# A WaveNet convolution on one core: a table of 663 moves applied to the planned instruction order

## The chip, the cores and the metric

The kernel runs on one core of a Trainium2 chip. Its time is device time in microseconds (us), given as the median of several runs. The engines have queues of their own and run in parallel: TensorE (PE, with its weight loads as PEld), VectorE (DVE), ScalarE (ACT), GpSimd (POOL) and SyncE (SP), which here only issues DMAs. Each queue runs in the order in which the program has its instructions; between queues there are semaphores.

## The reference

A causal dilated convolution (15 taps, dilation 2) of x (2 x 16000 x 144, bf16) to 288 channels, a gate, and a product with a 144 x 144 matrix:

```python
h = jnp.einsum('btc,cd->btd', xp[:, pad:pad + T, :], w[0])
for i in range(1, K):
    off = pad - i * dil
    h = h + jnp.einsum('btc,cd->btd', xp[:, off:off + T, :], w[i])
z = jnp.tanh(h[..., :D]) * _sigmoid(h[..., D:])
return z @ w_o
```

## The kernel before

**Tiling.** The 32000 rows are cut into 128 segments of 250, one to a partition, so that one matmul does one time step of all segments: a tile of 128 channels x 128 segments (XA) against 128 x 288 weights (WA, one per tap). The other 16 channels of eight taps are stacked in a second tile (XB, weights WB). Time steps are taken in groups of eight (octets).

**Fewer matmuls.** Sums and differences take the place of some of the products. DVE forms differences of the tiles in three levels (V, DU and DD from XA, BD from XB; `tt`, line 735) and over two octets (GX, GU, GV, GD; `g_diffs`, lines 809 to 821), and sums of the weights (WC, WS, WD, WV, WT; `wsum`, line 670). A unit is one parity of a pair of octets. Its matmuls are groups of two to four into one PSUM bank (line 827, all through the helper `region` or `mm`): CV, CD and XC make common parts, XR, SR and EF the parts of one octet, DD the ends. Between the groups ACT copies a bank to a second one (`copy`, line 976) or moves a pair of banks to SBUF as UD, UC or XS (`evict`, lines 477 and 480: one instruction if the two banks are neighbours, two if not). DVE adds UD (line 1003) and in EF the shared parts UE and UX to banks (line 1077; these are called the EF additions below), and POOL adds UC and XS to UX (line 1013).

**The end of a unit.** ACT takes Sigmoid and Tanh of a finished pair of banks into TG (`halves`, through `evict`), DVE multiplies them into Z (`gate`, line 854), SP transposes Z by DMA into ZT (`ship`, line 916), PE multiplies by w_o (WOR; `project`, line 933), ACT moves the result to OS (line 876) and SP stores it (line 944).

**Loads.** SP loads x in chunks (Xr, line 519). DVE or ACT copies 128 channels to STA, which SP transposes by DMA into XA (line 700). DVE copies the other 16 to C16 (line 686); SP transposes that to T16 (line 722), writes it to a DRAM scratch and builds XB from that and from the octet before (line 712).

**The start.** x and w come in pieces by SP (lines 519, 531); two small pieces for the first partition are issued by ACT. PE transposes the first x tiles (line 622), ACT and DVE move them to XA (line 628), DVE clears the first columns (line 636), ACT compacts the 16 channels into XBc (line 588), and PE computes the first eight steps directly (`direct`, tap by tap) while DVE makes the weight sums. ACT's queue begins with its DMA issues and a Sigmoid of a small zero tile SCR (line 564) that nothing reads.

**What sets the order.** All operations are entered in a graph (`_Graph.add`) with an engine, an estimated duration and the keys they read and write. `schedule` lays them out with a list scheduler ten times over, each time with due times from the pass before, and keeps the shortest plan: an order for each engine, and a PSUM bank for each bank object. The plan kept is that of the fourth pass. It has 977 operations on PE (2553 matmuls), 670 on ACT, 652 on DVE, 85 on POOL and 276 on SP. `assign` and `plan_waits` then turn dependencies into semaphores, and `emit` writes the queues.

Of the kernel before, what the change touches and what calls it, by code (L numbers as in the profile page):

```python
# [11 lines left out]
SEM_LAT = 0.05  # L12
DMA_LAT = 2.8
DMA_RATE = 280e3
MM = 0.122
PE_WIN = 42
ORDER = ("EF0 PJ EF1 XC1 CV CD0 DD00 DD01 DD10 CD1 XR1 XC0 DD11 UP0 XR0 SR0 PJ PJ SR1 UP1", "EF0 PJ EF1 XC1 CV CD0 CD1 XC0 DD00 SR0 XR0 SR1 XR1 UP0 UP1 DD01 DD10 DD11 PJ PJ")
LAT = {"pe": 0.17, "act": 0.12, "dve": 0.08, "pool": 0.1, "sp": 0.0}


class _Op:
# [46 lines left out]
class _Graph:  # L68
# [42 lines left out]
    def schedule(self, passes=10):  # L111

        users = {}
        for op in self.ops:
            for d in op.deps | op.soft:
                users.setdefault(d, []).append(op)
        best = None
        late, hint = {}, {}
        for _ in range(passes):
            span = self.run(users, late, hint)  # L120
            if best is None or span < best[0] - 1e-6:
                best = (span, dict((e, list(o)) for e, o in self.order.items()), [(op.start, op.end, op.bdeps, [b.phys for b in op.banks]) for op in self.ops])
            hint = dict((op, op.start) for op in self.ops)
            late = {}
            seq = {}
            extra = {}
            for a, b in zip(self.order["pe"], self.order["pe"][1:]):
                seq[a] = b
            for op in self.ops:
                for d in op.bdeps:  # L130
                    extra.setdefault(d, []).append(op)
            for op in sorted(self.ops, key=lambda o: -o.start):
                t = 1e9 if not (op.eng == "pe" or op in users) else span
                for u in users.get(op, ()):
                    if op in u.deps:
                        t = min(t, late[u] - self.lag(op, u))
                for u in extra.get(op, ()):
                    t = min(t, late[u] - self.lag(op, u))
                if op.eng == "pe":
                    t = min(t, late[seq[op]] - op.dur) if op in seq else min(t, op.start)  # L140
                late[op] = t
        self.order = best[1]
        for op, (a, b, c, d) in zip(self.ops, best[2]):
            op.start, op.end = a, b
            op.deps |= set(c)
            for bk, ph in zip(op.banks, d):
                bk.phys = ph
        return best[0]
# [4 lines left out]
    def run(self, users, late, hint):  # L153
        left = dict((op, len(op.deps | op.soft)) for op in self.ops)
        avail = dict((e, []) for e in self.ENGS)
        free = dict((e, 0.8) for e in self.ENGS)
# [4 lines left out]
        pool = []  # L161
        bleft = {}
# [6 lines left out]
        fixed = dict((b.phys, b) for b in bleft if b.fixed)  # L169
# [4 lines left out]
        dma_free = 0.0  # L174
        port = {"dve": 0.0, "pool": 0.0}
        ready = {}
# [3 lines left out]
        def make(op):  # L180
            t = 0.0
            for d in op.deps:
                t = max(t, d.start + d.dur if d.eng == op.eng == "pe" else d.end + SEM_LAT)
            for d in op.soft:
                t = max(t, d.start)
            ready[op] = t
            avail[op.eng].append(op)
# [61 lines left out]
        while n < len(self.ops):  # L249
# [24 lines left out]
            if op.opens:  # L274
                pool.sort(key=lambda x: x[:2])
                bd = set()
# [21 lines left out]
            for u in users.get(op, ()):  # L298
                left[u] -= 1
                if left[u] == 0:  # L300
                    make(u)
        return max(op.end for op in self.ops)

    def needs(self, op):
# [71 lines left out]
def _conv_wavenet_kernel(nc, x, w, w_o, out):  # L376
# [39 lines left out]
    with contextlib.ExitStack() as st:  # L416
# [891 lines left out]
        store_some(o1, [7], 1, 4, 4)  # L1308
        store_some(o1, [3], 1, 4, 0)

        _ms = g.schedule()
        nsem = [0]

        def mksem(name):
# [75 lines left out]
```

## Time and profile before

| | |
|---|---|
| median of 3 runs | 311.82 us (311.77 to 312.16) |
| the profiled execution | 310.92 us, span 309.2 us |
| granted TensorE clock | 0.998 |
| PE, DVE, ACT, POOL busy | 300.3, 289.7, 258.3, 101.3 us |
| matmuls | 2553 |
| DMA | 48.48 MB, mean 157 GB/s |

The span runs from the first to the last instruction of one profiled execution. A busy time is the union of an engine's instruction records, and records can overlap: a matmul's record (0.286 us for 288 columns) lasts longer than the time to the next one. Idle time ahead of an instruction is put down to whatever it waited for last. In the time line and the chain of waits each row has a start, a length in us, an engine (SPq is SP's queue of DMA issues), a line, an operation and the tiles out<-in.

### The profile page before, as it was taken

Reading aid. Unit: us, or ns where it says so; the run is one execution under the profiler, and the core shown is the slowest. Engines: PE = TensorE matmul, PEld = TensorE weight load, DVE = VectorE, ACT = ScalarE, POOL = GpSimd, SP = SyncE. Lnnn points to the kernel's source line nnn. Section 1 sums busy time; section 2 is a strip of 40 time slices with the busy share of each in tenths; the row PEclk is TensorE's granted clock in tenths of the full one; section 3 lists DMA queues with packets and bytes.
Section 4 is the critical chain, followed back from the end, with each engine's and each line's share of the span. In section 5 each row is a group of like instructions: output and inputs, shape, how many; then the busy total and the mean of one; then the engine's idle time right before and its main releaser. Section 6 shows DMA issues by size and latency. Waiting matters only on the chain.

```text
span 309.2 us, 7467 instructions
## 1 busy us (share of the span) xinstructions
PE 300.3 (97%) x2553; PEld 235.3 (76%) x2553; DVE 289.7 (94%) x652; ACT 258.3 (84%) x812; POOL 101.3 (33%) x89
## 2 busy tenths in 40 slices
PE   8899899999999999999999999999999999999995
PEld 7677576778787777877787777877878787777874
DVE  3899799999999999999999999999999999999864
ACT  3476598788889988888988888898888889988885
POOL 7660350333332233333222333321333332133330
PEclk9999999999999999999999999999999999999999
DMA  7958656748587575857557496977927693461353
GB/s 213 294 115 158 150 148 162 140 146 197 164 160 178 124 178 155 201 169 150 180 143 159 146 168 193 145 184 147 226 86 164 158 233 88 123 139 57 99 115 118
DMA packets 100386, 48.48 MB, mean 157 GB/s; under 512 B 88285, under 2 KB 91165, under 8 KB 100347
## 3 DMA queue, kind: packets, MB, share of 16 engines
q1 hardware_dynamic: 99801, 47.62, 63.6%
q0 software_dynamic: 512, 0.33, 0.5%
q8 instruction: 20, 0.33, 0.4%
q14 instruction: 19, 0.16, 0.2%
q10 hardware_dynamic: 34, 0.05, 0.1%
HBM read 13.77 MB, written 10.20 MB: 78 GB/s over the span
## 4 chain that ended last, share of the span: by engine, by line
PE 85%; DVE 6%; SPq 3%; DMA 2%; issue 1%; ACT 1%
PE PS L827 75%; PE PS L933 9%; DMA WA<-in_w_dram 1%; DMA XB<-s 1%; DVE V L735 1%; SPq L519 1%; SPq L712 1%; DVE PS L1077 1%; DVE DD L735 1%; SPq L722 1%; DVE DU L735 1%; ACT PS L976 0%; SPq L700 0%; DVE WC L670 0%; DVE WT L670 0%
## 5 line engine op out<-in xcount | busy, mean ns | idle before, releaser
L1013 POOL TENSOR_TENSOR UX<-UC,XS 128x576 f32<-128x576 f32 x60 | 85.2, 1441 | 194.2 <-ACT UC L477 141.7
L827 PE MATMUL PS<-WA,GD 128*128 128x288 bf16 x450 | 87.3, 286 | 0.5 <-DVE PS L1077 0.5
L976 ACT ACTIVATE PS<-PS 128x288 f32<-128x288 f32 x213 | 83.0, 439 | 0.6 <-PE PS L827 0.2
L827 PE MATMUL PS<-WB,BD 128*128 128x288 bf16 x240 | 67.5, 286 | 0.0
L477 ACT ACTIVATE TG<-PS 128x288 bf16<-128x288 f32 x148 | 52.8, 425 | 14.1 <-PE PS L827 13.9
L876 ACT ACTIVATE OS<-PS 128x432 bf16<-128x432 f32 (+1 forms) x93 | 42.0, 488 | 15.0 <-PE PS L933 14.6
L827 PEld LDWEIGHTS PS<-WA,GD 128*128 128x128 bf16 x450 | 42.6, 98 | 12.9 <-DVE PS L1077 1.4
L1077 DVE TENSOR_TENSOR PS<-PS,Xp 128x288 f32<-128x288 f32 x120 | 49.7, 457 | 1.6 <-PE PS L827 0.8
L1077 DVE TENSOR_TENSOR PS<-PS,UX 128x288 f32<-128x288 f32 x120 | 49.4, 454 | 0.0
L480 ACT ACTIVATE TG<-PS 128x144 bf16<-128x144 f32 x204 | 43.7, 312 | 5.9 <-PE PS L827 5.5
L1003 DVE TENSOR_TENSOR Xp<-PS,UD 128x576 f32<-128x576 f32 x60 | 42.6, 747 | 3.0 <-ACT UD L480 2.0
L827 PE MATMUL PS<-WS,GU 128*128 128x288 bf16 x210 | 44.7, 286 | 0.6 <-DMA XB<-s 0.4
L933 PE MATMUL PS<-WOR,ZT 128*128 128x144 bf16 (+1 forms) x322 | 38.5, 253 | 0.3 <-issue 0.3
L827 PE MATMUL PS<-WB,XB 128*128 128x288 bf16 x140 | 37.6, 286 | 0.0
L827 PE MATMUL PS<-WC,GV 128*128 128x288 bf16 x210 | 35.4, 287 | 0.7 <-ACT PS L976 0.7
L933 PEld LDWEIGHTS PS<-WOR,ZT 128*128 128x128 bf16 x322 | 27.2, 98 | 5.6 <-ACT XS L477 0.6
L827 PE MATMUL PS<-WD,DD 128*128 128x288 bf16 x210 | 31.1, 287 | 0.1
L854 DVE TENSOR_TENSOR Z<-TG 128x576 bf16<-128x576 bf16 (+1 forms) x63 | 27.4, 436 | 2.1 <-ACT TG L480 1.9
L827 PEld LDWEIGHTS PS<-WB,BD 128*128 128x128 bf16 x240 | 23.5, 98 | 5.8
L827 PEld LDWEIGHTS PS<-WS,GU 128*128 128x128 bf16 x210 | 20.0, 98 | 7.4 <-ACT PS L976 1.2
L827 PEld LDWEIGHTS PS<-WD,DD 128*128 128x128 bf16 x210 | 19.5, 98 | 7.1 <-ACT PS L976 2.2
L827 PE MATMUL PS<-WT,DU 128*128 128x288 bf16 x120 | 24.5, 286 | 0.0
(92 smaller groups left out, 470.1 us busy)
## 6 DMA issues: line engine op xcount, KB each, us to landing
Xr<-in_x_dram SPq DMA_DIRECT2D x15, 576.0 KB, 4.6
out_dram<-OS SPq DMA_DIRECT2D x30, 288.0 KB, 2.4
XB<-XB SPq DMA_DIRECT2D x30, 192.0 KB, 2.8
XB<-s SPq DMA_DIRECT2D x59, 32.0 KB, 1.9
s<-T SPq DMA_DIRECT2D x30, 32.0 KB, 3.5
WA<-in_w_dram SPq DMA_DIRECT2D x2, 288.0 KB, 4.5
ZT<-Z SPq DMA_TRANSPOSE x32, 2.9
Xp<-in_x_dram SPq DMA_DIRECT2D x2, 252.0 KB, 4.3
```

The costliest lines, as they stand in the source:

```text
L477: return e.activation(bass.AP(t[:].tensor, off + (0 if st > 0 else n), [[row, NP], [st, 2], [1, n]]), bass.AP(PS[:].tensor, lo * 512 + c0, ...
L480: ins = e.activation(bass.AP(t[:].tensor, off + i * n, [[row, NP], [1, n]]), bass.AP(PS[:].tensor, q.phys * 512 + c0, [[8 * 512, NP], [1, ...
L519: return e.dma_start(tile_ap, src)
L735: return g.add("dve", lambda v: v.tensor_tensor(dst(), a(), b(), ALU.subtract), r=r, w=wk, dur=dur, prio=2, lock=True)
L827: return lambda t: t.matmul(bank(b), lhsT=lhs(), rhs=rhs(), start=start, stop=True, skip_group_check=True)
L854: g.add("dve", lambda v: v.tensor_tensor(dst(), TG[:, s, 1, 2 * k:2 * k + n, :], TG[:, s, 0, 2 * k:2 * k + n, :], ALU.mult), r=[("TG", s, ...
L876: return (lambda e: e.activation(dst(), src(), ACT.Copy)) if eng == "act" else (lambda e: e.tensor_copy(dst(), src()))
L933: return t.matmul(PS[:, c0:c0 + n * D], lhsT=ZT[:, zt, blk_, :], rhs=WOR[:, wi_:wi_ + n, :].rearrange("p a b -> p (a b)"), start=first, st ...
L976: g.add("act", lambda e: e.activation(bank(c), bank(b), ACT.Copy), r=[("bank", b)], w=[("bank", c)], dur=0.29, prio=prio)
L1003: return v.tensor_tensor(ue(u % NU, q, 0, 2).rearrange("p (v n) -> p v n", v=2), src, UD[:, u % NUD, :, :], ALU.add)
L1013: op = g.add("pool", lambda p: p.tensor_tensor(UX[:, u % NU, h, :, :], UC[:, 0, :, :], bass.AP(XS[:].tensor, h * N2, [[2 * N2, NP], [0, 2] ...
L1077: g.add("dve", lambda e, dst=dst, src=src, ua=ua: e.tensor_tensor(bank(dst), bank(src), ua(), ALU.add), r=[("bank", src), ("UX", us, h) if ...
```

## The change

`schedule` runs five passes in place of ten, which includes the fourth, so that the plan to start from is the same. A new method `replay` takes a table with one list of numbers per engine. A pair "p q" takes the operation at place p out of that engine's queue and puts it in again at place q; pairs are applied one after the other: 198 on PE, 88 on ACT, 221 on DVE, 11 on POOL and 145 on SP. `replay` then walks through the queues in the new order with the estimated durations and deals the PSUM banks anew, taking neighbouring banks for a pair where it can. The dependencies through reused banks are now those of the new dealing. No operation is added or removed.

After the moves DVE's queue begins (with the place of before in brackets): 1 to 5 the first XA moves and clearings (2, 3, 6, 4, 8), 6 a sum WD<-WA (17), 7 V (10), 8 WS (7), 9 clearing (19), 10 WC (13), 11 WC (5), 12 WC (9), 13 V (21), 14 V (12), 15 WD (37), 16 WS (14), 17 WD (11). The three differences GX, GU and GV of the first pair of octets go from 57, 58 and 60 to 60, 63 and 65, among the two BD (64, 69 to 61, 71) and the first DU and V of the next octets. The operations up to place 75 are the same ones as before. On ACT the Sigmoid of SCR goes from place 3 to 24, behind the first `halves` (19 to 21), and the compaction copy of line 588 becomes the first activation, ahead of the second small DMA issue. On PE the last `direct` groups of the larger taps and some of the first `direct` groups are put off by up to 24 places, and the transposes of the last x piece and of XBc come earlier. On SP an XB copy (22 to 17) goes ahead of the first T16 transpose; later on stores and ZT transposes go back by up to eleven places and T16, STA and XB transfers come forward. Past the first 55 us most moves are by one place on PE and ACT, and by one to nine on DVE.

```diff
--- before.py
+++ after.py
@@ -12,10 +12,59 @@
 SEM_LAT = 0.05
 DMA_LAT = 2.8
 DMA_RATE = 280e3
+FIRST = (1.12, 1.1)
 MM = 0.122
 PE_WIN = 42
 ORDER = ("EF0 PJ EF1 XC1 CV CD0 DD00 DD01 DD10 CD1 XR1 XC0 DD11 UP0 XR0 SR0 PJ PJ SR1 UP1", "EF0 PJ EF1 XC1 CV CD0 CD1 XC0 DD00 SR0 XR0 SR1 XR1 UP0 UP1 DD01 DD10 DD11 PJ PJ")
 LAT = {"pe": 0.17, "act": 0.12, "dve": 0.08, "pool": 0.1, "sp": 0.0}
+MOVES = {
+    "pe": (
+        "6 5 7 12 8 7 10 15 12 11 19 16 18 21 18 39 26 20 22 28 22 46 22 41 23 22 24 36 29 24 25 29 25 28 25 27 30 47 30 42 30 37 35 30 36 31 40 32 34 48 34 43 "
+        "41 34 38 35 37 39 38 41 39 38 47 40 42 41 43 49 44 46 50 45 47 46 49 51 62 50 52 51 53 57 53 58 57 56 72 71 76 75 78 77 80 82 85 81 82 85 84 83 94 91 "
+        "97 96 99 98 101 100 103 102 107 106 108 110 117 115 118 116 124 127 128 131 130 129 132 137 136 135 154 153 171 170 174 173 195 194 200 197 201 200 "
...
+    ),
+    "act": (
+        "4 2 4 24 6 4 8 5 7 10 12 16 12 15 18 13 14 18 20 19 25 22 24 32 28 25 28 26 29 28 30 35 30 37 30 32 36 34 39 38 41 40 49 48 51 50 55 54 57 56 61 60 63 "
+        "62 68 67 70 69 73 72 75 74 76 78 79 81 91 90 97 96 104 103 112 111 118 117 125 124 139 138 154 153 181 180 191 190 215 214 223 222 232 234 238 237 275 "
...
+    ),
+    "dve": (
+        "1 27 5 3 5 11 5 8 16 6 7 12 18 9 10 17 10 14 12 10 20 13 14 16 37 15 16 26 18 17 19 21 20 29 22 20 37 22 32 23 24 31 45 25 26 30 28 27 29 50 30 29 36 "
+        "32 37 33 37 34 41 35 44 37 40 57 43 41 45 43 50 44 47 58 51 48 59 51 61 53 56 54 63 55 57 62 57 60 58 63 62 59 61 65 63 61 64 68 65 64 72 67 69 68 71 "
...
+    ),
+    "pool": (
+        "12 19 12 22 12 15 12 14 13 24 16 13 23 16 23 17 22 18 19 21 23 22 "
+    ),
+    "sp": (
+        "22 17 21 20 23 25 26 24 26 25 28 27 30 29 36 38 44 49 46 44 47 45 48 47 54 50 51 53 54 52 54 53 55 58 55 61 56 59 56 58 57 64 59 57 61 60 65 62 65 64 "
+        "68 78 68 70 71 69 71 70 75 73 79 75 78 82 83 79 81 80 82 85 83 86 87 84 87 86 88 91 88 92 93 90 92 96 94 93 95 100 96 95 101 97 100 98 100 102 106 101 "
...
+    ),
+}
 
 
 class _Op:
@@ -142,7 +191,6 @@
         self.order = best[1]
         for op, (a, b, c, d) in zip(self.ops, best[2]):
             op.start, op.end = a, b
-            op.deps |= set(c)
             for bk, ph in zip(op.banks, d):
                 bk.phys = ph
         return best[0]
@@ -299,6 +347,89 @@
                 left[u] -= 1
                 if left[u] == 0:
                     make(u)
+        return max(op.end for op in self.ops)
+
+    def replay(self, moves):
+
+        users = {}
+        for op in self.ops:
+            for d in op.deps | op.soft:
+                users.setdefault(d, []).append(op)
+        for e, text in moves.items():
+            seq, nums = self.order[e], [int(x) for x in text.split()]
+            for p, q in zip(nums[::2], nums[1::2]):
+                seq.insert(q, seq.pop(p))
+        left = dict((op, len(op.deps | op.soft)) for op in self.ops)
+        ready = dict((op, 0.0) for op in self.ops)
+        bleft, last, fixed = {}, {}, set()
+        for op in self.ops:
+            for b in op.banks:
+                bleft[b] = len(b.ops)
+                if b.fixed:
+                    fixed.add(b.phys)
+                else:
+                    b.phys = None
+        pool = [(0.0, ph, None) for ph in range(8) if ph not in fixed]
+        free = dict((e, 0.8) for e in self.ENGS)
+        port = {"dve": 0.0, "pool": 0.0}
+        pos = dict((e, 0) for e in self.ENGS)
+        dma_free = 0.0
+        for _ in range(len(self.ops)):
+            pick = None
+            for e in self.ENGS:
+                if pos[e] == len(self.order[e]):
+                    continue
+                op = self.order[e][pos[e]]
+                if left[op] or len(pool) < len(op.opens):
+                    continue
+                t = max(free[e], ready[op])
+                if op.opens:
+                    pool.sort(key=lambda x: x[:2])
+                    t = max(t, pool[len(op.opens) - 1][0])
+                elif op.lock:
+                    t = max(t, port["pool" if e == "dve" else "dve"])
+                if pick is None or t < pick[0]:
+                    pick = (t, e, op)
+            assert pick, "the moves leave no order"
+            st, e, op = pick
+            pos[e] += 1
+            op.start = st
+            if op.lock:
+                port[e] = st + op.base
+            bd = set()
+            for b in op.opens:
+                can = [i for i, q in enumerate(pool) if q[0] <= st + 1e-9] or [0]
+                free_ph = set(pool[i][1] for i in can)
+                if b.mate is not None and b.mate.phys is not None:
+                    good = [i for i in can if abs(pool[i][1] - b.mate.phys) == 1]
+                elif b.mate is not None:
+                    good = [i for i in can if pool[i][1] - 1 in free_ph or pool[i][1] + 1 in free_ph]
+                else:
+                    good = [i for i in can if pool[i][1] - 1 not in free_ph and pool[i][1] + 1 not in free_ph]
+                _, b.phys, old = pool.pop((good or can)[0])
+                if old is not None:
+                    bd.update(old.ops)
+            op.bdeps = bd
+            op.dur, op.lat = op.base, op.base + LAT[op.eng]
+            if op.pair and len(op.banks) == 2 and abs(op.banks[0].phys - op.banks[1].phys) != 1:
+                op.dur += 0.07
+                op.lat += 0.07
+            free[e] = st + op.dur
+            if op.dma:
+                dma_free = max(dma_free, st + op.dur) + op.nbytes * (FIRST[0] if op.quick else 1.0) / DMA_RATE
+                op.end = dma_free + DMA_LAT - (FIRST[1] if op.quick else 0.0)
+            else:
+                op.end = st + op.lat
+            for b in op.banks:
+                last[b] = max(last.get(b, 0.0), op.end)
+                bleft[b] -= 1
+                if bleft[b] == 0:
+                    pool.append((last[b] + SEM_LAT, b.phys, b))
+            for u in users.get(op, ()):
+                left[u] -= 1
+                ready[u] = max(ready[u], op.start if op in u.soft and op not in u.deps else op.start + op.dur if op.eng == u.eng == "pe" else op.end + SEM_LAT)
+        for op in self.ops:
+            op.deps |= set(op.bdeps)
         return max(op.end for op in self.ops)
 
     def needs(self, op):
@@ -1308,7 +1439,8 @@
         store_some(o1, [7], 1, 4, 4)
         store_some(o1, [3], 1, 4, 0)
 
-        _ms = g.schedule()
+        g.schedule(5)
+        _ms = g.replay(MOVES)
         nsem = [0]
 
         def mksem(name):
```

26 rows, old and new, of the table MOVES are left out of this document.

## Prediction

> **What bounds the kernel now.** First the page, for the shares; then the windows view, for where the two full engines idle; then the chain, the time lines and the waits for what each idle time waits on.
>
> ```profile
> span 309.2 us, 7467 instructions
> PE 300.3 (97%) x2553; PEld 235.3 (76%) x2553; DVE 289.7 (94%) x652; ACT 258.3 (84%) x812; POOL 101.3 (33%) x89
> PE 85%; DVE 6%; SPq 3%; DMA 2%; issue 1%; ACT 1%
> ```
>
> PE is busy 97% of the span and is 85% of the chain that ended last. VectorE (DVE) is at 94%, nearly as full. The change removes no instruction of either, so all that it can win is idle time, and all that it can lose is new idle time. The windows view says where idle time is (start:end, length, then busy time and instructions of PE, PEld, DVE, ACT, POOL):
>
> ```profile
> 0.00:9.07 9.07, 7.79 (x80) 6.69 (x80) 2.50 (x13) 3.48 (x8) 5.92 (x10) 1.00 0.78 220
> 9.07:37.57 28.50, 25.73 (x217) 19.19 (x215) 26.36 (x64) 17.43 (x40) 11.97 (x20) 1.00 0.73 174
> 37.57:55.00 17.43, 16.42 (x132) 11.87 (x131) 16.98 (x36) 15.19 (x51) 6.74 (x5) 1.00 0.63 158
> 55.00:165.00 110.00, 110.00 (x931) 86.81 (x930) 108.99 (x243) 96.78 (x311) 35.07 (x26) 1.00 0.67 164
> 165.00:175.00 10.00, 9.87 (x84) 7.63 (x82) 10.00 (x23) 8.80 (x34) 2.77 (x2) 1.00 0.56 173
> 175.00:290.00 115.00, 115.00 (x973) 90.62 (x972) 113.68 (x249) 102.51 (x325) 35.17 (x26) 1.00 0.65 147
> 290.00:304.00 14.00, 14.00 (x132) 11.25 (x130) 9.80 (x27) 12.38 (x43) 3.66 (x3) 1.00 0.35 87
> 304.00:309.20 5.20, 1.47 (x21) 1.21 (x18) 1.37 (x4) 1.74 (x5) 0.00 (x0) 0.86 0.46 172
> ```
>
> PE idles 1.28 us up to 9.07, 28.50 - 25.73 = 2.77 up to 37.57, 1.01 up to 55, then 0.13 in the whole of 55 to 304, and 3.73 at the end. So 250 of the 309 us have no PE idle time to win. A short stall can hide in a busy row, because a matmul's record is longer than its place in the queue. The chain repeats two stretches in the steady part, one of 61 matmuls and one of 55, and these show how much that is:
>
> ```profile
> 118.41 7.52 PE PS L827 x61
> 172.69 7.70 PE PS L827 x61
> ...
> 200.38 6.74 PE PS L827 x55
> 272.24 6.86 PE PS L827 x55
> ```
>
> The same work differs by 0.18 and 0.12 us at most between its repeats. With some 26 such stretches and most of them within 0.06 of the shortest, I estimate about 0.8 us of hidden stalls from 55 to 304.
>
> DVE idles 28.50 - 26.36 = 2.14 us from 9.07 to 37.57, then 0.45, 1.01, 0.00 and 1.32 up to 290. It too is almost never free, and the pipeline cannot start before DVE's chain of weight sums and differences is through. Its queue in the start, with the two stalls that matter (start, length, engine, line, operation, [idle before]):
>
> ```profile
> 6.06 0.30 DVE L670 TENSOR_TENSOR WC<-WA 128x288 bf16<-128x288 bf16 x1
> 6.29 0.29 DVE L670 TENSOR_TENSOR WS<-WA 128x288 bf16<-128x288 bf16 x1
> 6.52 0.29 DVE L670 TENSOR_TENSOR WC<-WC,WA 128x288 bf16<-128x288 bf16 x1
> 6.73 0.28 DVE L735 TENSOR_TENSOR V<-XA 128x256 bf16<-128x256 bf16 x1
> 6.93 0.30 DVE L670 TENSOR_TENSOR WD<-WA 128x288 bf16<-128x288 bf16 x1
> 7.15 0.28 DVE L735 TENSOR_TENSOR V<-XA 128x256 bf16<-128x256 bf16 x1
> 9.07 0.46 DVE L670 TENSOR_TENSOR WC<-WA 128x576 bf16<-128x576 bf16 x1 [1.64 <-DMA WA<-in_w_dram]
> ...
> 31.97 0.42 DVE L735 TENSOR_TENSOR DU<-XA 128x512 bf16<-128x512 bf16 x1 [0.70 <-DMA XA<-STA]
> 34.10 0.69 DVE L735 TENSOR_TENSOR BD<-XB 128x1024 bf16<-128x1024 bf16 x1 [0.80 <-DMA XB<-s]
> 34.71 0.46 DVE L1077 TENSOR_TENSOR PS<-PS,Xp 128x288 f32<-128x288 f32 x1
> 36.34 1.22 DVE L1077 TENSOR_TENSOR PS<-PS,Xp 128x288 f32<-128x288 f32 x3
> ```
>
> **The change, part by part.** The profiled execution took 310.92 us with a span of 309.2; the median of the three runs is 311.82, 0.90 more. I work the sum against 310.92 and add the 0.90 at the end.
>
> *DVE's queue in the start (moves 5->11, 16->6, 37->15, 45->25 and their neighbours).* A WD sum that reads the third piece of WA goes to place 6. In the time line that piece lands at 9.07, so DVE now waits there. Behind it are the six sums and differences that ran from 6.06 to 7.43 while the piece was on its way. So 7.43 - 6.06 = 1.37 us of DVE work moves from before the landing to after it. Up to the third of the first EF additions (36.34, place 75 before and after) DVE has the same operations in both orders. From 9.07 to there it was busy 26.36 and idle 2.14; it now has 26.36 + 1.37, and it is earlier only by what it saves of the 2.14: at best 2.14 - 1.37 = 0.77. For that it must lose the waits of 0.70 and 0.80. I think it does: the differences GV, GU and GX, which stood ahead of these waits, now stand among them (places 58 to 65), so DVE comes to each load later in its work and finds it landed. I take -0.7. The ends are -0.77 (no idle time left) and +1.37 (all 2.14 stay).
>
> *PE's queue in the start.* It has three stalls ahead of the first EF, and two in the filling of the pipeline:
>
> ```profile
> 9.84 0.61 PE L622 MATMUL PS<-ID,Xp 128*128 128x128 bf16 x8 [0.56 <-DMA Xp<-in_x_dram]
> 11.06 4.83 PE L827 MATMUL PS<-WA,XA 128*128 128x288 bf16 x38 [0.61 <-DVE XA L636]
> 23.19 0.91 PE L827 MATMUL PS<-WC,V 128*128 128x288 bf16 x6 [0.43 <-ACT PS L976]
> 34.13 0.42 PE L827 MATMUL PS<-WS,GU 128*128 128x288 bf16 x2 [0.40 <-DMA XB<-s]
> ...
> 47.16 0.42 PE L827 MATMUL PS<-WA,GD 128*128 128x288 bf16 x2 [0.25 <-DVE PS L1077]
> 54.31 0.54 PE L827 MATMUL PS<-WC,GV 128*128 128x288 bf16 x3 [0.67 <-ACT PS L976]
> ```
>
> The moves 19->16 and 26->20 put direct matmuls and a later group of transposes into the first two, and 62->50 a DU group into the third. PE then reaches the region of 31 some 1.6 us sooner. That is worth nothing by itself: the groups there read GX, GU and GV, which DVE now makes later (places 60, 63, 65), and the second XB load, which lands at 34.1. So what PE wins before 31 it waits for after it, and the first EF additions move by DVE's term alone. I cost these moves at 0 beyond it. If DVE did not hold it back, PE could win all of 2.77.
>
> *The filling, 37.57 to 55.* PE's idle time is 1.01, of which 0.25 + 0.67 = 0.92 are two waits on places in other queues. At 47.16 it waits for an EF addition, and the moves 117->115 and 118->116 put two DD groups ahead of two EF groups there. At 54.31 it waits for a copy on ACT behind two evictions, and 76->78, 79->81 and 132->137 reorder ACT and PE there. A row of 38 matmuls in 4.83 us is 0.127 each with the last one's tail, and a single record lasts 0.29, so each of the two hides up to 0.16 more: 0.92 + 0.32 = 1.24, with the rest some 1.4. I take -1.0, between 0 and -1.4: the moves stand at these two places, but a stall that goes leaves the next queue's head to be waited for.
>
> *The steady part, 55 to 304.* Some 130 of PE's 198 moves swap neighbours here (a DD, CD, EF or SR group one place earlier), with matching moves on ACT. The idle time to win is 0.13 and the hidden stalls about 0.8. DVE has 2.33 idle there, so it could follow. Against it, every swap is fitted to a plan and could make a stall where there is none. I take -0.3, between -0.8 and +1.0 (a stall such as the 0.25 at 47.16 in four of the units).
>
> *ScalarE's first function.* Move 4->24 takes the small Sigmoid of line 564 from ahead of all other activations to place 24, behind the first real Sigmoid.
>
> ```profile
> 2.11 1.28 ACT L564 ACT_TABLE_LOAD   x1 [2.11 <-issue]
> 3.41 0.23 ACT L564 ACTIVATE SCR<-SCR 128x32 bf16<-128x32 bf16 x1
> 4.21 0.31 ACT L588 ACTIVATE XS<-Xp 128x128 bf16<-128x128 bf16 x1 [0.58 <-DMA Xp<-in_x_dram]
> ...
> 21.21 1.62 ACT L477 ACTIVATE TG<-PS 128x288 bf16<-128x288 f32 x5 [1.38 <-PE PS L827]
> 30.22 0.71 ACT L477 ACTIVATE TG<-PS 128x288 bf16<-128x288 f32 x2 [1.98 <-PE PS L827]
> ```
>
> The one table load of the program stands directly ahead of its first activation, in time that ACT had free. Now the first activation is the copy of line 588, which waits for x until 4.21, and the load may come only after that wait: 1.28 us more for the eviction behind it, which PE's direct groups read next. If what is loaded for a copy holds no Sigmoid, a second load stands ahead of the first Sigmoid (21.21 in this trace). I cost both at 0: the first is covered by PE's later wait for x (0.56 + 0.61), the second by ACT's waits for PE (1.38 and 1.98). Without that cover each costs up to 1.28. The Trainium skill's page "ScalarE: Activation LUTs", section "Table sets: the hidden batching unit", says that cheap functions sit in every set while each set has one expensive anchor, which speaks against this move, since a copy then need not bring Sigmoid along. Its section "What ACT_TABLE_LOAD costs" puts a switch at 1.28 us and 1.38 of drain; by that the whole sum would be 0.7 us above zero if nothing hid it. The trace agrees on the 1.28 and shows no drain (the activation follows 0.02 us after the load); a second load no row here shows.
>
> *The rest.*
>
> ```profile
> 12.25 8.55 POOL L1213 DMA_DIRECT2D WOR<-in_w_o_dram  x16 [0.27 <-DMA WA<-in_w_dram]
> 36.22 0.41 PE L933 MATMUL PS<-WOR,ZT 128*128 128x144 bf16 x3 [0.32 <-issue]
> ```
>
> POOL's 11 moves reorder sixteen loads that are all issued by 20.8 and first read at 36.22: 0. SP's 145 moves put the stores later and the transposes (T, XA) and XB loads earlier. In the start an XB copy goes ahead of the first T transpose and waits there for ScalarE's XB eviction; that eviction is moved up as well, so I cost it at 0, and its worst is inside the +1.37. The tail past 304 keeps its work: 0. An eviction from two banks takes one instruction if the banks are neighbours and two if not, and the banks are dealt anew; no row says how, so it stands as part of the +1.0.
>
> The sum: -0.7 - 1.0 - 0.3 = -2.0. That is 308.9 for a profiled execution and, with the 0.90, **309.8** as median.
>
> **The rivals.** (1) *PE is not held by DVE.* The deferred matmul groups fill the wait for XB, and PE loses its idle time from 9.07 on: 2.77 + 1.01 + 0.13 = 3.91, so 307.9, and down to 306.5 with the hidden stalls. For it: PE is 85% of the chain. Against: GX, GU and GV come later on a full DVE. (2) *The table loads land on the path.* One of 1.28 uncovered on top of the forecast: 311.1. For it: PE already waits 0.43 for ACT at 23.19. Against: ACT's 1.98 of waiting soon after. (3) *Slower: DVE starts its chain late.* The wait for WA at place 6 leaves 1.37 us of work behind, the waits on XA and XB stay because SP's chain is no earlier, and the first EF additions and all behind them come 1.37 later: 313.2. It decides as soon as DVE's idle time from 9.07 to those additions stays above 0.77. (4) *The table changes nothing that counts*: 250 us have no idle time to win, and what the start wins is waited for again: 311.8.
>
> **How the numbers follow.** Forecast 0.38 (308.9 to 310.6), rival 1 0.20, rival 2 0.17 (310.6 to 311.7), rival 3 0.20 (312.5 to 314.5), rival 4 0.05. The measurement can tell about 0.2%, 0.62 us, from no change. Faster by that means below 311.2: the forecast, rival 1 and half of rival 2, 0.66. Within it: the other half and rival 4, 0.14. Slower: 0.20. For 8 in 10 the range has to reach into rival 1 and rival 3: 306.8 to 313.4 leaves out the lower part of the one and the upper part of the other, some 0.15.
>
> **What would show it.** In the profile after, DVE should idle from about 6.6 to 9.07, then hardly at all up to the first EF additions, which should start near 35.6 instead of 36.34. PE's waits of 0.56, 0.61 and 0.43 should be gone, and a longer one stand ahead of its first GU or GV group. From 55 on PE should stay without idle rows, and the last matmul come 2 us sooner. I am wrong if the EF additions come later than 36.3 (rival 3), if a second table load is followed by a PE wait on ACT (rival 2), or if PE reaches them without waiting (rival 1).

## The result and the profile after

| | before | after |
|---|---|---|
| median (6 runs each) | 311.79 us (310.70 to 312.62) | 309.18 us (308.45 to 309.61) |
| ratio of after to before, 95% interval | | 0.9915 [0.9891, 0.9939] |
| the profiled execution | 310.92 us, span 309.2 | 308.45 us, span 306.4 |

The change makes the kernel 2.6 us faster; the forecast was 309.8 (306.8 to 313.4). The profiled executions differ by 2.47, and the one of after is its fastest of six.

Of the page of after, the span, the busy times and the chain of waits by engine:

```profile
span 306.4 us, 7439 instructions
PE 299.6 (98%) x2553; PEld 235.2 (77%) x2553; DVE 289.5 (94%) x652; ACT 260.0 (85%) x799; POOL 99.6 (33%) x89
PE 88%; ACT 4%; DVE 2%; DMA 2%; SPq 2%; issue 1%; DVEq 0%
```

The work is the same. Of the 2.8 us of span, 2.1 are idle time of PE (309.2 - 300.3 = 8.9 before, 306.4 - 299.6 = 6.8 after), and 0.7 was hidden in its busy time. PE's share of the chain rises from 85 to 88%, DVE's falls from 6 to 2%. ACT has 13 instructions fewer (812 before): 14 evictions less are split in two, and there is one table load more. The windows view (start:end, length, busy time and instructions of PE, PEld, DVE, ACT, POOL), with the cut of 37.57 moved to 36.50, since the pipeline starts that much sooner:

```profile
0.00:9.07 9.07, 7.69 (x77) 6.84 (x78) 2.09 (x9) 2.84 (x4) 5.93 (x10) 1.00 0.79 216
9.07:36.50 27.43, 25.94 (x221) 19.32 (x219) 26.70 (x68) 19.51 (x48) 11.47 (x21) 1.00 0.73 176
36.50:55.00 18.50, 17.99 (x146) 12.90 (x146) 18.22 (x40) 15.76 (x54) 7.13 (x5) 1.00 0.74 168
...
301.00:306.40 5.40, 1.93 (x25) 1.43 (x23) 1.70 (x5) 1.78 (x6) 0.00 (x0) 0.88 0.43 164
```

PE's idle time is now 1.49 in the start after 9.07 (2.77 before) and 0.51 in the filling (1.01). DVE is busy for 26.70 of 27.43. The time line of DVE in the start, at the places quoted for before:

```profile
8.19 0.46 DVE L801 TENSOR_TENSOR WD<-WA 128x576 bf16<-128x576 bf16 x1 [1.25 <-DMA WA<-in_w_dram]
...
33.36 0.47 DVE L1208 TENSOR_TENSOR PS<-PS,Xp 128x288 f32<-128x288 f32 x1 [0.27 <-PE PS L958]
...
35.20 1.18 DVE L1208 TENSOR_TENSOR PS<-PS,Xp 128x288 f32<-128x288 f32 x3
```

DVE waits for WA as forecast, and the waits of 0.70 on XA and 0.80 on XB are gone. The row of EF additions that the prediction goes by starts at 35.20 instead of 36.34 (it is the second of the four, where the prediction says the third). But the piece of WA landed at 8.19, 0.88 earlier than in the trace of before, and no move touches its load. From landing to second addition it is 27.01 against 36.34 - 9.07 = 27.27 before: behind the landing the order won 0.26 in these two traces. The time line of PE, its rows with idle time ahead of the first EF:

```profile
12.85 1.15 PE L958 MATMUL PS<-WA,XA 128*128 128x288 bf16 x8 [0.36 <-DVE XA L767]
20.85 0.53 PE L958 MATMUL PS<-WC,V 128*128 128x288 bf16 x3 [0.29 <-ACT PS L1107]
31.97 0.30 PE L958 MATMUL PS<-WS,GU 128*128 128x288 bf16 x1 [0.31 <-ACT PS L1107]
35.71 0.42 PE L958 MATMUL PS<-WA,GD 128*128 128x288 bf16 x2 [0.42 <-DVE PS L1208]
```

Of the three stalls of 0.56, 0.61 and 0.43 the first is gone and the other two are 0.36 and 0.29. The longer wait that I expected ahead of GU is 0.31; it seems that the groups that were put off fill most of it.

For the parts further on busy time is too coarse, so here is a measure that the text uses from now on. **Lost time** is the sum, over successive matmuls, of the time between their starts beyond the spacing that the shape has when nothing holds it (0.1225 us for 288 columns, 0.0625 for 144, 0.0555 for a transpose, read off undisturbed stretches). It is worked out from the starts of all 2553 records and shows the hidden stalls too.

| lost time of PE, us | 37.5 to 60 | 60 to 300 |
|---|---|---|
| before | 1.86 | 1.85 |
| after | 1.31 | 0.71 |

Between these two traces the filling won 0.55 and the steady part 1.1. A coarser look says the same; the windows view for 55 to 300, before and then after:

```profile
55.00:300.00 245.00, 244.87 (x2068) 192.94 (x2067) 238.99 (x527) 217.15 (x699) 76.52 (x56) 1.00 0.64 153
```

```profile
55.00:300.00 245.00, 245.00 (x2079) 193.82 (x2077) 239.80 (x530) 219.10 (x690) 75.08 (x55) 1.00 0.66 153
```

Eleven more matmuls start in the same 245 us; at 245 / 2079 = 0.118 each that is 1.3 us. ACT does it with 690 instructions instead of 699.

Last, ScalarE's table loads, in the time line of ACT:

```profile
4.23 1.28 ACT L719 ACT_TABLE_LOAD   x1 [4.23 <-DMA Xp<-in_x_dram]
5.52 0.31 ACT L719 ACTIVATE XS<-Xp 128x128 bf16<-128x128 bf16 x1
...
17.96 0.41 ACT L608 ACTIVATE TG<-PS 128x288 bf16<-128x288 f32 x1
18.39 1.28 ACT L608 ACT_TABLE_LOAD   x1
19.69 0.71 ACT L608 ACTIVATE TG<-PS 128x288 bf16<-128x288 f32 x2
```

Both loads that the prediction had thought of came: the first only after the wait for x, the second between the first gate function and the next. In this execution the second even stands on the chain of waits.

### The profile page after: what moved, and what is told of

Read it like the earlier page. It is cut to its first block, busy times and chain, and to the rows that moved or that the text cites. A ratio compares the mean times of both kernels' runs of the same rounds, so it can differ in the third digit from the quotient of the medians.

```text
span 306.4 us, 7439 instructions
## 1 busy us (share of the span) xinstructions
PE 299.6 (98%) x2553; PEld 235.2 (77%) x2553; DVE 289.5 (94%) x652; ACT 260.0 (85%) x799; POOL 99.6 (33%) x89
## 4 chain that ended last, share of the span: by engine, by line
PE 88%; ACT 4%; DVE 2%; DMA 2%; SPq 2%; issue 1%; DVEq 0%
PE PS L958 78%; PE PS L1064 9%; DMA WA<-in_w_dram 1%; SPq L650 1%; DMA XB<-s 1%; ACT TG L608 1%; ACT STA L826 1%; ACT PS L1107 1%; ACT TG L611 1%; ACT XB L792 0%; ACT L608 0%; PE PS L1024 0%; SPq L853 0%; SPq L843 0%; DVE WC L801 0%
## 5 line engine op out<-in xcount | busy, mean ns | idle before, releaser
L1144 POOL TENSOR_TENSOR UX<-UC,XS 128x576 f32<-128x576 f32 x60 | 83.8, 1417 | 191.5 <-ACT UC L608 130.4
L1107 ACT ACTIVATE PS<-PS 128x288 f32<-128x288 f32 x213 | 80.9, 429 | 2.6 <-PE PS L958 2.3
L608 ACT ACTIVATE TG<-PS 128x288 bf16<-128x288 f32 x164 | 58.3, 423 | 7.0 <-PE PS L958 6.5
L1007 ACT ACTIVATE OS<-PS 128x432 bf16<-128x432 f32 (+1 forms) x93 | 43.1, 489 | 17.0 <-PE PS L1064 15.4
L958 PEld LDWEIGHTS PS<-WA,GD 128*128 128x128 bf16 x450 | 41.8, 98 | 14.1 <-DVE PS L1208 2.0
L611 ACT ACTIVATE TG<-PS 128x144 bf16<-128x144 f32 x172 | 36.9, 304 | 5.7 <-PE PS L958 5.4
L1064 PE MATMUL PS<-WOR,ZT 128*128 128x144 bf16 (+1 forms) x322 | 41.0, 253 | 0.0
L958 PE MATMUL PS<-WC,GV 128*128 128x288 bf16 x210 | 36.5, 286 | 0.2 <-ACT PS L1107 0.2
L958 PE MATMUL PS<-WD,DD 128*128 128x288 bf16 x210 | 32.5, 286 | 0.0
```

Of the source, the lines that this page charges most:

```text
L608: return e.activation(bass.AP(t[:].tensor, off + (0 if st > 0 else n), [[row, NP], [st, 2], [1, n]]), bass.AP(PS[:].tensor, lo * 512 + c0, ...
L611: ins = e.activation(bass.AP(t[:].tensor, off + i * n, [[row, NP], [1, n]]), bass.AP(PS[:].tensor, q.phys * 512 + c0, [[8 * 512, NP], [1, ...
L958: return lambda t: t.matmul(bank(b), lhsT=lhs(), rhs=rhs(), start=start, stop=True, skip_group_check=True)
L1007: return (lambda e: e.activation(dst(), src(), ACT.Copy)) if eng == "act" else (lambda e: e.tensor_copy(dst(), src()))
L1064: return t.matmul(PS[:, c0:c0 + n * D], lhsT=ZT[:, zt, blk_, :], rhs=WOR[:, wi_:wi_ + n, :].rearrange("p a b -> p (a b)"), start=first, st ...
L1107: g.add("act", lambda e: e.activation(bank(c), bank(b), ACT.Copy), r=[("bank", b)], w=[("bank", c)], dur=0.29, prio=prio)
```

## The experiments

Twelve kernels, each timed 5 to 12 times beside before. They ran in three sets, on a chip each: the parts, the single moves, and the kernels with other banks. The median of before was 311.7, 311.9 and 311.6 in them, so kernels of different sets are compared by their ratios. The theory (T) was the one of the prediction: the start, the filling and the steady part win separately, and the new dealing of banks costs or wins little. The first rival was that something goes with the dealing, the second that single moves in the start carry the gain.

A number of use throughout is how many evictions are **split**, that is, find their two banks not neighbours and take two ACT instructions. Counted in the traces, it is 144 before, 147 in e_empty and 130 after (an expectation below gives 147 for before, which is the count of e_empty).

| kernel | split | ACT instr. | median us | ratio to before, 95% |
|---|---|---|---|---|
| e_empty | 147 | 815 | 311.77 | 0.9998 [0.9982, 1.0014] |
| e_start | 170 | 839 | 313.11 | 1.0042 [1.0025, 1.0059] |
| e_fill | 166 | 834 | 311.46 | 0.9991 [0.9980, 1.0003] |
| e_steady | 194 | 862 | 312.79 | 1.0038 [1.0023, 1.0052] |
| e_start_fill | 171 | 840 | 310.76 | 0.9964 [0.9951, 0.9978] |
| e_start_banks | 116 | 785 | 312.34 | 1.0022 [1.0011, 1.0033] |
| e_steady_banks | 125 | 793 | 311.20 | 0.9993 [0.9973, 1.0012] |
| e_split_more | 196 | 865 | 311.12 | 0.9979 [0.9958, 1.0000] |
| e_sig_first | 130 | 798 | 309.29 | 0.9924 [0.9905, 0.9942] |
| e_wd_back | 130 | 799 | 308.82 | 0.9901 [0.9881, 0.9921] |
| e_both | 130 | 798 | 308.99 | 0.9909 [0.9888, 0.9929] |
| e_late_sig | 147 | 816 | 311.87 | 0.9999 [0.9982, 1.0016] |

### The parts one by one

Each list is cut at the places of about 37 and 55 us (PE 88 and 145, ACT 45 and 85, DVE 75 and 110, SP 40 and 66; POOL's moves all belong to the start), and only one part is kept. e_empty keeps none, so that only the banks are dealt anew.

```diff
 MOVES = {
-    "pe": ( ... 198 pairs ...
+    "pe": ( only the pairs of the part; e_empty: " "
```

> The empty table: the plan of before, with the banks dealt anew by the walk through the queues. The theory expects no difference that can be measured from before, 311.2 to 312.4, with the start, the waits near 47 and 54 us and the steady part as before. The rival of the banks expects a gain of 1 us or more here, with fewer ScalarE instructions in the line of two-instruction evictions.

> Only the moves up to the first EF additions (PE places below 88, ACT 45, DVE 75, SP 40, all of POOL): 142 of the 663. The theory (three separate gains: start, filling, steady part) expects the additions at L1208 near 35.2 us as with the whole table, a last matmul 1.1 us sooner than before, and a time of 310.7. The rival that the gain comes from the new dealing of the PSUM banks expects the time of the whole table, 309.2, or that of the empty table, whatever the moves.

> Only the moves between the first EF additions and about 55 us: 55 of the 663. The theory expects 0.5 to 1.0 us less than before, 311.0, with the PE waits near 47 and 54 us shorter and all of the start as before. The rival (the wait at 54 us comes from the start's lateness) expects no gain without the start's moves, 311.8.

> Only the moves past 55 us: 466 of the 663. The prediction's term was -0.3; the two traces put the PE time lost between matmuls from 60 to 300 us at 1.9 before and 0.7 after, so the theory now expects -1.2, 310.6. The rival, that those hidden stalls went with the banks or with the better start, expects 311.5 or more.

The new dealing alone changes nothing in the time (0.9998), as T had it. The rest did not come as T had it: against 311.7 the start costs 1.4, the filling wins 0.25 (its interval holds no change), and the steady part costs 1.1. The sum is 2.2 **slower**, and the whole is 2.6 faster. So as times they are not three separate gains. In the profile of e_start the EF additions that were expected at 35.2 start at 36.16 (WA landed at 9.26 there). The waits view shows one reason for the start (window 37 to 60; engine, tile, line <- what it waited for: us in total, times, longest), in e_start:

```profile
PEld PS L931 <- DVE PS L1181: 2.7, 3, 1.1
PE PS L931 <- DVE PS L1181: 1.8, 3, 0.8
```

Line 1181 are the EF additions. With the new start and the old queues behind it PE waits for them in the filling (the two rows overlap, since a matmul and its weight load wait together; lost time 3.84 against 1.86 before and 2.74 in e_empty). For the steady part alone the waits view shows another engine; window 60 to 300, before, e_steady and after:

```profile
PEld PS L827 <- ACT PS L976: 2.9, 14, 0.4
```

```profile
PEld PS L944 <- ACT PS L1093: 4.8, 20, 0.4
```

```profile
PEld PS L958 <- ACT PS L1107: 1.1, 5, 0.3
```

These are PE's waits for `copy`. e_steady has the order of after there and waits four times as long. What differs is the dealing, with 194 splits and 862 ACT instructions against 130 and 799, and whatever stands ahead of 55 us.

### The start's single moves

e_sig_first is the whole table with the first Sigmoid ahead of all activations as before; e_wd_back puts the six short weight sums and V differences ahead of the WD sum that waits for WA; e_both does both; e_late_sig has, of the whole table, only the late Sigmoid.

```diff
 e_sig_first:  act + "3 2 24 3"    dve + "27 1"
 e_wd_back:    dve + "11 6 9 7 12 8 10 9 17 10 15 11"
 e_late_sig:   act = "4 2 4 24"    dve = "1 27"    all others " "
```

> The whole table, but ScalarE's queue begins as before: the small Sigmoid (and its DVE clearing) ahead of the copy of x. One table load near 2.1 us, none near 18.4. The theory that both loads are covered expects no change from the whole table, 309.2 within 0.6, with PE's wait for a copy near 20.3 us (0.45) smaller or gone and the time given back before the first EF additions, which stay near 35.2. The rival, that the loads cost on the path, expects up to 1.28 us less, 307.9.

> The whole table, but DVE runs the six short sums and differences ahead of the WD sum that waits for the third piece of WA, as before. DVE then has 1.37 us less to do after that piece has landed. The theory, that DVE's chain sets the first EF additions, expects them up to 1.37 us sooner, near 34.0, and a time up to 1.3 less, 308.0. The rival, that the XB loads by way of SP set them, expects them near 35.2 still, and 309.2.

> Both of these edits on the whole table. If both costs are on the path, they add up: 306.8. If ScalarE's loads are covered and DVE's chain is what counts, 308.0, as with the DVE edit alone. If neither is, 309.2.

> The empty table, with the copy of x ahead of the small Sigmoid and that Sigmoid at place 24 of ScalarE's queue: the table load's two places in an order that is otherwise that of before. The theory that ScalarE's free time covers both loads expects the time of the empty table, 311.8. The rival that they land on the path expects 1.28 more, 313.1; the wait of 0.43 for a copy at 23.19 would then be some 1 us longer.

**The loads cost nothing that shows.** e_sig_first has one load, e_late_sig two; ACT's time line of e_sig_first:

```profile
2.11 1.28 ACT L690 ACT_TABLE_LOAD   x1 [2.11 <-issue]
...
18.90 1.01 ACT L603 ACTIVATE TG<-PS 128x288 bf16<-128x288 f32 x3
```

The three gate functions run in one piece, and the time is 309.29 against 309.18 with both loads. The same pair with the short sums first, e_both and e_wd_back, is at 308.99 and 308.82. The other way round e_late_sig has 0.9999 and e_empty 0.9998, and its wait for a copy, which was expected to grow by 1 us, is 0.53 against 0.42 in e_empty. The intervals of each pair leave room for some 0.7 to 0.9 us, less than one load. That the load was on the chain of one execution did not make it worth 1.28: other waits take its place.

**The wait for WA costs at most a little, and varies.** DVE's time lines of e_sig_first and then of e_wd_back:

```profile
9.50 0.46 DVE L796 TENSOR_TENSOR WD<-WA 128x576 bf16<-128x576 bf16 x1 [2.29 <-DMA WA<-in_w_dram]
...
36.20 1.19 DVE L1203 TENSOR_TENSOR PS<-PS,Xp 128x288 f32<-128x288 f32 x3
```

```profile
8.98 0.46 DVE L796 TENSOR_TENSOR WD<-WA 128x576 bf16<-128x576 bf16 x1 [0.30 <-DMA WA<-in_w_dram]
...
34.79 0.76 DVE L1129 TENSOR_TENSOR Xp<-PS,UD 128x576 f32<-128x576 f32 x1 [0.28 <-PE PS L953]
35.46 1.18 DVE L1203 TENSOR_TENSOR PS<-PS,Xp 128x288 f32<-128x288 f32 x3
```

With the WD sum first, the additions follow the landing by 36.20 - 9.50 = 26.70 here and by 27.01 in after. With the short sums first it is 35.46 - 8.98 = 26.48. In e_both it is 35.88 - 9.42 = 26.46. So taking the 1.37 us of work out from behind the landing brings the additions some 0.5 closer to it, not 1.37. What stops them is in the second trace: DVE waits for PE, and PE's time line there says for what.

```profile
33.84 0.42 PE L953 MATMUL PS<-WS,GU 128*128 128x288 bf16 x2 [0.33 <-DMA XB<-s]
```

It is the XB load, which SP issued at 31.23 in e_wd_back and at 31.05 in after (31.44 in before). In these traces DVE's chain and SP's chain end within a few tenths of each other; after's own chain of waits, too, runs through the XB load issued at 31.05. The time of e_wd_back is 308.82, the best measured, but its interval and that of after overlap: the two are not told apart. e_both does not add the two edits up either: 308.99, where that had meant 306.8.

### Banks and parts together

Now the banks were taken by themselves. e_split_more has the order of after and takes the last fitting bank in place of the first; the other two have the order of a part alone and a dealing with few splits, taken from a table of choices; e_start_fill has the start and the filling together.

```diff
 e_split_more:
-                _, b.phys, old = pool.pop((good or can)[0])
+                _, b.phys, old = pool.pop((good or can)[-1])
 e_start_banks, e_steady_banks:
-                _, b.phys, old = pool.pop((good or can)[0])
+                cho = good or can
+                _, b.phys, old = pool.pop(cho[deal.get(nth, 0) % len(cho)])
```

> The whole table in its order, with one edit in the dealing of banks: of the free banks that fit, the walk takes the one freed last in place of the one freed first. 196 evictions of a pair of banks then need two ScalarE instructions in place of 130. The theory that the parts lost because of the dealing (170 and 194 such evictions with the start's and the steady part's moves alone, 147 before) expects most of the gain to go, 310.7 or more, with PE waiting on ScalarE. The theory that the order counts, and the parts are fitted to each other, expects 309.2 to 309.8.

> The moves past 55 us alone, in the same order as in the run of that part, with the banks dealt so that 125 evictions need two instructions in place of 194. The theory of the dealing expects the part's gain to come out: 310.6, and the time lost between matmuls from 60 to 300 us to fall from 2.8 to 0.7. The theory of the order expects 312.8 still.

> The moves up to the first EF additions alone, in the same order as in the run of that part, with 116 evictions of two instructions in place of 170. The theory of the dealing expects 311.0 or less. The theory of the order, that DVE's queue behind the start is now the wrong one for where DVE stands, expects 313.1 still, with PE waiting on DVE's EF additions between 37 and 60 us.

> The moves up to about 55 us (start and filling, 197 of the 663), banks dealt by the unchanged walk (171 evictions of two instructions). The theory of the order expects PE's lost time from 37.5 to 60 us to fall from 3.8, as with the start alone, to the 1.3 of the whole table, and 310.8: the filling's moves put DVE's queue right for the new start. The theory of the dealing expects nearly the time of the start alone, 312.5 or more.

**The dealing carries much of the gain.** e_split_more has after's order on every engine, and 66 splits more. It takes 311.12: of the 2.6 us it loses 1.9. The groups view of it, for the length of a whole eviction and of a piece of a split one (ahead of the last bar: busy, mean ns):

```profile
L603 ACT ACTIVATE TG<-PS 128x288 bf16<-128x288 f32 x114 | 42.1, 429 | 5.6 <-PE PS L953 5.3
L606 ACT ACTIVATE TG<-PS 128x144 bf16<-128x144 f32 x272 | 56.4, 322 | 7.0 <-PE PS L953 6.6
```

One record of 0.43 becomes two of 0.32, but records overlap. From start to start, back to back, a whole takes 0.305 and a piece 0.171 (medians), so a split costs ACT 2 x 0.171 - 0.305 = 0.04 of queue time. That fits its busy time, which grows by only 2.7 for the 66 (262.7 against 260.0, still 85%). My reading is that PE waits longer where such pieces stand ahead of a `copy` that it needs. The waits view of e_split_more, 60 to 300, against 1.1 in after:

```profile
PEld PS L953 <- ACT PS L1102: 4.1, 18, 0.3
```

and its windows view from 55 to 300, with 2065 matmuls where after has 2079:

```profile
55.00:300.00 245.00, 244.96 (x2065) 191.14 (x2063) 238.74 (x525) 220.11 (x740) 75.92 (x55) 1.00 0.66 153
```

e_steady_banks shows it from the other side: the steady part alone, with 125 splits in place of 194, goes from 312.79 to 311.20, and PE's waits for `copy` from 4.8 to 2.0.

```profile
PEld PS L968 <- ACT PS L1117: 2.0, 10, 0.3
```

That takes back all that the steady part alone had cost, but it is no gain over before (0.9993). What the two kernels with another dealing change is the whole dealing: which evictions are split, and also which bank waits for which. The price of a split by itself is not isolated by them.

**The start needs the filling's order, not banks.** e_start_banks has only 116 splits. It is some 0.6 us better than e_start (1.0022 against 1.0042), but still slower than before, at 312.34. Its waits view, 37 to 60:

```profile
PEld PS L956 <- DVE PS L1206: 2.7, 3, 1.1
PE PS L956 <- DVE PS L1206: 2.2, 4, 0.8
```

They are the waits of e_start, hardly changed. With the filling's 55 moves added and 171 splits, e_start_fill takes 310.76, and of these waits this is left:

```profile
PEld PS L933 <- DVE PS L1183: 0.8, 3, 0.4
```

By the ratios start and filling together win 1.1 of the 2.6 us, and the steady moves with the banks that come with them the other 1.5.

**Where each part wins and loses.** The traces of all kernels, by stretch, with the splits that fall into the last one:

| lost time of PE, us | order past 55 us | 37.5 to 60 | 60 to 300 | splits from 60 to 300 |
|---|---|---|---|---|
| before | old | 1.86 | 1.85 | 130 |
| e_empty | old | 2.74 | 1.65 | 130 |
| e_start | old | 3.84 | 2.50 | 145 |
| e_start_banks | old | 3.69 | 1.77 | 98 |
| e_fill | old | 1.73 | 2.39 | 148 |
| e_start_fill | old | 1.32 | 2.31 | 152 |
| e_steady | new | 2.78 | 2.78 | 179 |
| e_steady_banks | new | 2.47 | 1.02 | 109 |
| e_split_more | new | 1.94 | 1.97 | 167 |
| after | new | 1.31 | 0.71 | 115 |

Against e_empty, which has the old order and the same rule of dealing, the filling's moves take 1.0 off in their own stretch without the new start (2.74 to 1.73), and the steady moves take 0.6 off in theirs where few evictions are split (1.65 to 1.02 in e_steady_banks; e_start_banks, with fewer splits still and the old order, has 1.77). The start brings the EF additions nearer to WA's landing (26.90 in e_start, 27.76 in e_empty). What undoes this in the time of e_fill and e_start stands further on, where they moved nothing: 0.7 and 0.85 more from 60 to 300, with 148 and 145 splits in place of 130, and for e_start 1.1 more in the filling. So the parts do win in their own stretches. What does not add up is what a part does behind itself, through DVE's place in its queue and through the dealing. From 60 to 300 the old order loses 1.65 to 1.85 with up to 130 splits and 2.31 to 2.50 with 145 to 152, the new one 0.71 to 1.02 with 109 to 115 and 1.97 to 2.78 with 167 and more. That speaks for the splits as the way in which the dealing acts, though it does not prove it. One caution: the filling of before has 1.86 and the three kernels with its order there and a new dealing 2.47 to 2.78, yet the time of e_empty is that of before; one trace each does not say why.

## Why the prediction was right, and where it was not

**What bounds the kernel** held: all that was won is waiting of PE, 2.1 us of it visible as idle time and 0.7 hidden in busy rows. In the steady part nearly all of it was hidden.

**DVE's queue in the start (-0.7).** The mechanism was right (WD waits for WA, the waits for XA and XB go in after, the EF additions come sooner). In the profiles they came 1.14 sooner, but 0.88 of that is WA's landing, which is luck: in the traces of all kernels it lies between 8.19 (after) and 9.50 (e_sig_first). From the landing to the second addition it is 26.51 to 28.02, mean 27.51, in the six kernels with the old start and 26.70 to 27.28, mean 26.97, in the six with this one. That is some 0.5, with groups that overlap, so the term was of the right kind and somewhat too large. What it left out is a second bound: e_wd_back and e_both moved the work back, and the XB load by way of PE held the additions instead. Rival 3 did not come, since DVE lost its 1.5 us of waits; its price of 1.37 counts the moved work in full, and the 0.5 of e_wd_back makes that look too high as well.

**PE's queue in the start (0 beyond DVE's term).** Right in the sum: PE waits 0.42 for DVE ahead of the EF group at 35.71. It had less to wait out before that than I thought, it seems because it worked on deferred groups. Rival 1, PE free of DVE with 307.9, did not come.

**The filling (-1.0).** Lost time there fell by 0.55 between before and after, inside the range given. As repairs of the old stalls the moves do win 1.0 there (e_fill against e_empty), but 0.7 of it is lost again further on, and the time of e_fill is at most 0.6 below before. What I did not see is that they are also the follow-up of the new start: with it they take away 2.5 us (3.84 to 1.32).

**The steady part (-0.3, -0.8 to +1.0).** This is the term that was mis-sized: -1.1 by lost time, beyond the range on the winning side. The estimate of 0.8 for the hidden stalls looked only inside the repeated stretches. The quickest of those lose nothing (0.00 in the stretch of 61 at 118.41); much of the 1.85 from 60 to 300 stands between them, 0.29 of it ahead of one group at 169.2. And I put the new dealing of banks down only as a part of the +1.0. It was a gain: 14 splits fewer than before, 41 fewer than what the start and the filling leave with the plain dealing. From 60 to 300 e_split_more loses 1.26 more than after with 52 splits more; at that rate the 37 that e_start_fill has more than after there are worth 0.9 of the 1.6 between these two. By the rows of the old order, 2.31 with 152 splits and 1.65 to 1.85 with 130, it is nearer 0.5. Both are estimates that take splits to be alike and to be the cause; the rest, 0.7 to 1.1, would be the order.

**The table loads (0).** Right: both came, and both are covered. Rival 2 with its 1.28 is out by e_sig_first and e_late_sig, to within the 0.3% of these comparisons. The Trainium skill's page "ScalarE: Activation LUTs", section "What ACT_TABLE_LOAD costs", adds a drain to the 1.28; it shows in no row here: the activation starts 0.02 us after the second load.

**The tail (0).** From the last matmul's start to the end it is 3.63 us against 3.95, but the lost time from 300 to that matmul is 0.29 against 0.05. The end as a whole is nearly level.

So the 2.0 came out near the measured 2.6 with terms that were off both ways: between the two profiles the start behind the landing won 0.26 where 0.7 was forecast, the filling 0.55 for 1.0 and the steady part 1.1 for 0.3. Those three make 1.9, and the early landing of WA in the profile of after most of the rest. The sum was better than its terms, and part of that is luck. One figure of the rivals does not follow from the rows: 0.8 of hidden stalls off 307.9 gives 307.1, not 306.5.

What stays open: why e_start_banks, with the filling's old order, waits just at those places and not at others was not followed through DVE's queue operation by operation. How the last step's gain divides between order and banks is an estimate, since no run had after's order with a dealing of exactly e_start_fill's quality, and none changed the splits without changing which bank waits for which. And whether e_wd_back is better than after would take more runs.

## What to carry to other kernels

A reordering that was fitted as a whole has to be read as a whole: here every part alone was level or slower in time, and trying parts one by one would have condemned all of them. A trace of a part, read stretch by stretch, shows what it wins in its own place and what it spoils behind itself. When queues are reordered, count what the order changes in the resources dealt out behind it (here, pairs of banks that are not neighbours), and look at which engine the full engine's small waits end on. A wait that is on the chain of one trace is worth its length only if nothing else ends shortly after it; move it and look again.

## What the runs showed of the hardware

- An activation that reads two neighbouring banks at once has a record of 0.43 us for 288 columns, one that reads 144 from one bank 0.32 (mean of 114 and 272, e_split_more). Back to back they start 0.305 and 0.171 apart (medians), so two pieces in place of a whole cost 0.04 of ACT's time. The dealing with 66 more of them cost 2.7 us of ACT's busy time and 1.9 us of the kernel, though ACT is busy only 85%.
- The table load stands directly ahead of the first activation and, where that one waits, behind its wait (at 4.23 in after, for x; at 2.11 in e_sig_first, without a wait). In after one of the two gate functions ran under the first set, and the next needed a second load (18.39).
- The same load of WA, which SP issued between 4.24 and 4.69 us in all fourteen profiled kernels, had its first reader on DVE start anywhere between 8.19 and 9.50: over a microsecond that a profile of one execution can show as gain or loss.
